# Attention and channel mix on one core: the scheduler books GpSimd with VectorE for some instructions, splits w_k out of PSUM and gets new prices

## The chip, the core and the metric

The kernel runs on one core of a Trainium2 chip. The metric is device time in microseconds (us) of the whole program, as the median of several runs. Engines are named as in the profile: PE is TensorE (PEld its weight load), DVE is VectorE, ACT is ScalarE, POOL is GpSimd, SP is SyncE, which only issues DMAs here. PSUM is the memory into which PE writes and which POOL's instructions in this kernel never touch; SBUF is the large one.

## What is computed

Causal attention with a forgetting bias, and behind it a channel mix with squared ReLU and a gate. Shapes: 8 batches, 8 heads, 576 positions, head width 64; model width 512, hidden width 1024.

```python
# attention, per batch and head
scores = scale * np.matmul(q, k.transpose(0, 1, 3, 2))
cum = np.cumsum(np.maximum(s, 0.0), axis=-1)
bias = -(cum[:, :, :, None] - cum[:, :, None, :])
scores = np.where(causal, -1e9, scores + np.minimum(bias, 0.0))
attn = np.exp(scores - max); attn = attn / (sum(attn) + 1e-09)
x = attn @ v                       # heads side by side: 512 wide
# channel mix on x
xk = mu_k * x + (1 - mu_k) * x_prev
xr = mu_r * x + (1 - mu_r) * x_prev
k = np.maximum(xk @ w_k, 0.0)
v = k * k @ w_v
out = v / (1 + np.exp(-(xr @ w_r)))
```

## The kernel before

**Precision.** Large products are made as sums of products of float16 parts: each operand is split into a high part and a low part (what the high part leaves), and three products (high by high, high by low, low by high) stand for one float32 product. The splits are the work of DVE, ACT and POOL around each product.

**Stages.** A visit is one batch and one pair of heads. The first eight visits treat batch 0 in two halves (four early visits A, then four Z); batch 1 follows in the same plain manner (`scores`, `turn_plain`, `sum_plain`), and from batch 2 on `split_scores`, `turn_by_dma` (weights are transposed by DMA) and `sum_values` are used. Between visits stand the 18 chunks of the channel mix (`channel_mix`, 256 tokens each): `hidden` (line 1954, products with w_k, then ReLU at 1968, and squares), `gate` (line 2031, products with w_r, tanh at 2045, scale at 2050) and `output` (line 2076, products with w_v, the last product with the gate at 2087).

**Squares.** In the first six chunks `hidden` makes kh = r*r (rounded) on ACT, squares r in place in float32 on ACT (line 1985) or on DVE (line 1990), and makes the low part kl on DVE from kh and r, both in SBUF (line 1996). In later chunks the exact square stays in PSUM (lines 2012 and 2018), so DVE's instruction for kl reads one operand from SBUF and one from PSUM.

**Weights.** The weights come as float64 words and are put together in `load_weight`: POOL extracts bits (lines 863, 871), ACT writes a first form to PSUM (878), DVE takes its maximum (883) and then writes the float32 weight to an SBUF tile `whole` (890; the tile's storage is named xrh or xrl). `split` makes the high part on ACT (901) or POOL (906) and the low part on DVE (914) or, in two instructions, on POOL (920 and 924); for w_v a third part, on ACT (933) or DVE (938). w_k has 8 such blocks, w_r 4, w_v 8.

**What sets the order.** Nothing is executed in the order of the source. Every instruction is added to a `Plan` with an engine, a price in ns, what it reads and writes, and a due time; `or_act`, `or_dve` and `or_pool` name a second engine for it. `forward` lays all instructions out on a clock of its own, engine by engine, taking for a free engine the ready instruction with the earliest due time; `backward` turns the result into new due times; this is repeated 60 times and the best layout is emitted. Each engine then executes its instructions strictly in that order, and real waits are made by semaphores. So a price never changes what an instruction costs on the chip; it changes where it stands and, with a second engine, on which it runs. For SP `forward` keeps a clock of the DMA rings (`moved`): FIRST and `land` are latencies, AHEAD says how far issue may run ahead of the transfers. While PE would have nothing to do early on, `one_idle` (line 464) puts dummy products in its queue.

## Time and profile before

| what | value |
|---|---|
| median of 3 runs | 773.28 us (772.52 to 773.45) |
| the profiled execution's own time | 774.11 us |
| its span, first to last instruction | 772.2 us |
| PE busy | 738.4 us, 96% |
| DVE, ACT, POOL busy | 607.2, 577.4, 504.1 us (79, 75, 65%) |
| matmuls | 5384 |
| instructions recorded | 16996 |

The profiled execution is one run; 1.9 us of its time lie outside the span. Busy time of PE is the union of its instructions with ends that are modelled, so that two matmuls that follow each other closely overlap; a PE that is shown busy can still be waiting for weights. The granted clock is a share of TensorE's full 2.4 GHz. In a view of waits, the engine and line named behind the arrow are what ended the idle time.

### The profile page before, as it was taken

The numbers are of one execution on the slowest core, as the hardware profiler recorded it, in microseconds if no ns is written. First come the engines' busy times: TensorE is split into PE (matmuls) and PEld (weight loads), VectorE is DVE, ScalarE is ACT, GpSimd is POOL, SyncE is SP. The second block draws the span as 40 slices with busy tenths as digits, with TensorE's granted clock in tenths as the row PEclk, the third lists the DMA queues.
The fourth block names the chain that finished last, engine by engine and source line by source line (L and its number), as shares of the span: only waits on it lengthen the run. The fifth ranks groups of instructions, "written<-read, shape, count | busy, mean of one in ns | idle before, by whom it ended". The sixth has DMA issues, their size and how long they took to land.

```text
span 772.2 us, 16996 instructions
## 1 busy us (share of the span) xinstructions
PE 738.4 (96%) x5384; PEld 492.7 (64%) x5384; DVE 607.2 (79%) x1820; ACT 577.4 (75%) x1751; POOL 504.1 (65%) x615
## 2 busy tenths in 40 slices
PE   8989998999899989999999999999999999999998
PEld 7867765765557555757575756575656666755665
DVE  8989978889878999888989898889998878413321
ACT  6989987878979897887888887988887777312311
POOL 6899999697365698777976887588758941100000
PEclk9999999999999999999999999999999999999999
DMA  8856672368258879788878788888787664200000
GB/s 269 259 180 185 198 216 95 99 158 179 71 104 185 176 170 159 158 174 168 174 175 167 177 174 166 163 173 177 173 144 163 105 115 65 67 28 14 14 28 27
DMA packets 207336, 109.91 MB, mean 142 GB/s; under 512 B 178000, under 2 KB 183888, under 8 KB 207248
## 3 DMA queue, kind: packets, MB, share of 16 engines
q1 hardware_dynamic: 207248, 108.85, 61.9%
q8 instruction: 42, 0.69, 0.4%
q14 instruction: 46, 0.38, 0.1%
HBM read 54.09 MB, written 12.24 MB: 86 GB/s over the span
## 4 chain that ended last, share of the span: by engine, by line
PE 37%; DVE 16%; ACT 15%; issue 6%; DMA 1%; POOL 1%; DVEq 0%; ACTq 0%; POOLq 0%
PE m L2076 10%; PE m L1954 7%; PE m L2031 5%; DVE W L1354 4%; ACT t L1323 3%; ACT W L1348 3%; PE pair L1482 3%; PE s L1296 2%; ACT s L1323 2%; DVE t L1308 2%; PE t L1296 2%; ACT wd L1527 2%; DVE s L1308 2%; PE s L1954 2%; PE t L1954 2%
## 5 line engine op out<-in xcount | busy, mean ns | idle before, releaser
L1954 PEld LDWEIGHTS <-w_k 128*128 128x128 f16 x1728 | 161.7, 98 | 37.7 <-issue 12.1
L1954 PE MATMUL m<-xkh,w_k 128*128 128x256 f16 x976 | 180.7, 275 | 2.5 <-DVE kl L2018 1.4
L2076 PE MATMUL m<-w_v,kh 128*128 128x512 f16 x528 | 167.9, 383 | 1.3 <-POOL w_v L924 0.7
L1954 PE MATMUL m<-xkl,w_k 128*128 128x256 f16 x488 | 134.3, 275 | 1.0 <-DVE xkl L1926 0.5
L2076 PE MATMUL m<-w_v,kl 128*128 128x512 f16 x264 | 100.2, 381 | 0.8 <-DVE kl L1996 0.7
L1143 POOL TENSOR_TENSOR KH<-raw,KH 64x576 fp32r<-64x576 f32 x64 | 93.5, 1461 | 4.7
L2076 PEld LDWEIGHTS <-kh 128*128 128x128 f16 x592 | 56.7, 98 | 57.7 <-issue 4.7
L2031 PE MATMUL m<-w_r,xrh 128*128 128x512 f16 x264 | 87.2, 386 | 2.6 <-ACT r L1968 1.3
L1167 POOL TENSOR_TENSOR QL<-raw,G 64x576 fp32r<-64x576 f32 (+1 forms) x64 | 86.2, 1347 | 3.3
L2050 POOL TENSOR_SCALAR g<-g,scale 128x512 f32<-128x512 f32 x26 | 20.8, 799 | 102.6 <-ACT g L2045 90.2
L1323 ACT ACTIVATE s<-s,nm 128x64 f32<-128x64 f32 (+2 forms) x144 | 61.5, 427 | 26.0 <-DVE nm L1308 20.7
L1296 PE MATMUL s<-KH,G 128*128 128x64 f32 (+3 forms) x192 | 68.8, 360 | 9.0 <-DVE W L1354 7.8
L1163 POOL CAST G<-raw 128x576 fp32r<-128x576 f32 x48 | 32.9, 686 | 65.1 <-issue 35.5
L1354 DVE SCALAR_TENSOR_TENSOR W<-s,rinv,W 128x64 f16<-128x64 f32 (+2 forms) x144 | 65.2, 456 | 11.4 <-ACT W L1348 10.0
L1348 ACT ACTIVATE W<-s,rinv 128x64 f16<-128x64 f32 (+2 forms) x144 | 65.0, 455 | 11.4 <-DVE rinv L1339 9.5
L1296 PE MATMUL s<-KL,QL 67*128 67x64 f32 (+3 forms) x192 | 66.5, 351 | 0.0
L1354 DVE SCALAR_TENSOR_TENSOR W<-t,rinv,W 128x320 f16<-128x320 f32 (+1 forms) x96 | 61.7, 646 | 5.6 <-ACT W L1348 4.9
L1323 ACT ACTIVATE t<-t,nm 128x320 f32<-128x320 f32 (+1 forms) x96 | 55.4, 577 | 7.2 <-DVE nm L1385 4.2
L1348 ACT ACTIVATE W<-t,rinv 128x320 f16<-128x320 f32 (+1 forms) x96 | 57.8, 608 | 2.2 <-DVE rinv L1339 2.1
L1308 DVE CUSTOM_DVE_ANT_0 t<-t,lower 128x320 f32<-128x320 f32 (+1 forms) x96 | 57.1, 599 | 1.9 <-PE t L1296 1.4
L1968 ACT ACTIVATE r<-m 128x512 f32<-128x512 f32 x57 | 34.1, 599 | 27.4 <-PE m L1954 21.8
L1482 PE MATMUL pair<-T,V 128*64 128x512 f16 (+6 forms) x768 | 54.4, 295 | 0.0
(260 smaller groups left out, 1968.5 us busy)
## 6 DMA issues: line engine op xcount, KB each, us to landing
raw<-in_q SPq DMA_DIRECT2D x112, 144.0 KB
raw<-in_k SPq DMA_DIRECT2D x32, 288.0 KB
vn<-in_v SPq DMA_DIRECT2D x24, 384.0 KB
out<-g SPq DMA_DIRECT2D x35, 256.0 KB
wd<-in_moe_w_v SPq DMA_DIRECT2D x8, 512.0 KB
T<-W SPq DMA_TRANSPOSE x192
V<-in_v SPq DMA_DIRECT2D x8, 320.0 KB
wd<-in_moe_w_k SPq DMA_DIRECT2D x4, 512.0 KB
```

Of the source, the lines that this page charges most:

```text
L1143: lambda own=own, other=other, K=K: nc.gpsimd.tensor_tensor(out=K.get()[other], in0=k.get()[own], in1=f32(K.get()[own]), op=ALU.subtract),
L1167: lambda x=x, QQ=QQ, QL=QL: nc.gpsimd.tensor_tensor(out=QL.get()[0:64, 0:nq], in0=x.get()[0:64], in1=f32(QQ.get()[0:64]), op=ALU.subtract,),
L1296: lambda x=x, G=G, K=K, r=r: nc.tensor.matmul(ps.get()[:m, :n], G.get()[:r, q : q + m], K.get()[:r, k0 : k0 + n], start=x == 0, stop=x == 1,),
L1308: lambda: nc.vector.tensor_tensor_reduce(out=ps.get()[:, :n], in0=ps.get()[:, :n], in1=mask(), scale=-SCALE, scalar=3.0e38, op0=ALU.add, o ...
L1323: lambda: nc.scalar.activation(ps.get()[:, :n], ps.get()[:, :n], AF.Exp, bias=nm.get()[:, i + o : i + o + 1], scale=-1.0, accum_out=sums.g ...
L1348: lambda: nc.scalar.activation(part(0), ps.get()[:, :n], AF.Copy, scale=rinv.get()[:, i : i + 1]),
L1354: lambda: nc.vector.scalar_tensor_tensor(out=part(1), in0=ps.get()[:, :n], scalar=rinv.get()[:, i : i + 1], in1=part(0), op0=ALU.mult, op1 ...
L1482: nc.tensor.matmul(ps.get()[64 * j : 64 * j + 64, a:e], V.get()[:, block[0], block[1], j], moving(j), start=first, stop=last, tile_positio ...
L1954: lambda u=u, f=f, c=c, n=n, w=w, x=x: nc.tensor.matmul(ps.get()[:, u * CT : (u + 1) * CT], weight["k", c, f // 4].get()[:, w, f % 4 * P : ...
L1968: lambda: nc.scalar.activation(r.get(), ps.get(), AF.Relu, scale=2.0**-26),
L2031: lambda c=c, n=n, x=x, w=w: nc.tensor.matmul(ps.get(), row(1, x, c, place + tt * P, place + tt * P + P), weight["r", c, 0].get()[:, w], s ...
L2076: lambda f=f, i=i, x=x, w=w, ps=ps, columns=columns: nc.tensor.matmul(ps.get()[:, 0:n], x.get()[:, f, ts], weight["v", f, 0].get()[:, w, c ...
```

## The change

The change leaves the arithmetic as it is, except in where w_k's float32 form is kept. It does five things.

1. `forward` gets a set `shared` of DVE instructions that read two operands from SBUF or run SBUF to SBUF in a fast mode. When one of them is next and POOL is booked (`free["POOL"] > s`), up to DEPTH ready DVE instructions are compared by due time plus the time that POOL is still booked, and the best goes first. A shared instruction then starts no earlier than POOL is free, and books POOL for its own length.
2. The members of that set lose the flat surcharge that stood for this before: line 1996 and 1990 had 400 ns, 914 had 450 ns.
3. For w_k the float32 form is written back to the PSUM bank (890), and both parts are split from there by ACT and DVE; POOL is no longer an alternative for w_k.
4. Prices of DMAs fall: plain transfers from 1.286 to 1.05 times the given ns, a transposing DMA from 195 to 155 ns a block, `land` from 1300 to 1150; ISSUE, FIRST and AHEAD are changed.
5. Prices of some DVE and ACT instructions are changed by tens of ns up to 130 ns.

```diff
-    ISSUE, FIRST, AHEAD = 500.0, 1000.0, 2500.0
+    ISSUE, FIRST, AHEAD = 520.0, 900.0, 3500.0
...
+        self.shared = set()
...
+            if e == "DVE" and i in self.shared and free["POOL"] > s:
+
+                some, aside = [(due[i], i)] if own == e else [], []
+                while some and ready[e] and len(some) < self.DEPTH:
+                    x = heapq.heappop(ready[e])
+                    if on[x[1]]:
+                        continue
+                    (some if self.tasks[x[1]][0] == e else aside).append(x)
+                    if len(aside) > 2:
+                        break
+                if some:
+                    best = min(
+                        some,
+                        key=lambda x: x[0]
+                        + (self.LOCK * (free["POOL"] - s) if x[1] in self.shared else 0.0),
+                    )
+                    for x in some + aside:
+                        if x is not best:
+                            heapq.heappush(ready[e], x)
+                    i = best[1]
...
+            if e == "DVE" and i in self.shared:
+                s = max(s, free["POOL"])
+                free["POOL"] = s + ns
...
+    LOCK = 1.0
...
-        return plan.add("SP", 1.286 * ns, emit, reads, writes, land=1300)
+        return plan.add("SP", 1.05 * ns, emit, reads, writes, land=1150)
...
-        whole = whole_in_ring(x) if name == "v" else wholes()
+        in_bank = name == "k"
+        whole = ps if in_bank else whole_in_ring(x) if name == "v" else wholes()
...
+            if in_bank:
+                act(
+                    lambda: nc.scalar.activation(
+                        block.get()[:, 0], ps.get(), AF.Copy, scale=unit_at
+                    ),
+                    [ps, key], [hi], 512, 94,
+                )
+                dve(
+                    lambda: nc.vector.scalar_tensor_tensor(
+                        out=block.get()[:, 1], in0=ps.get(), scalar=unit_at,
+                        in1=block.get()[:, 0], op0=ALU.mult, op1=ALU.subtract,
+                    ),
+                    [ps, key, hi], [lo], 512,
+                )
+                return
...
-            or_pool(dve(low, [whole, key, hi], [lo], 512, extra=450), low_in_two, 512, 1551)
+            or_pool(dve(low, [whole, key, hi], [lo], 512, extra=125, both=True), low_in_two, 512, 1551)
...
-        i = plan.add("SP", 195.0 * blocks, emit, reads, writes, land=1000)
+        i = plan.add("SP", 155.0 * blocks, emit, reads, writes, land=1000)
...
-                [lower, (corners_mask, 0), (corners_mask, 1)], [ps, (nm, i)], n, extra=78,
+                [lower, (corners_mask, 0), (corners_mask, 1)], [ps, (nm, i)], n, extra=137,
...
-                    2 * CT, 400,
+                    2 * CT, 75, both=True,
...
-                    [r, (kh, fp)], [(kl, fp)], 2 * CT, extra=400,
+                    [r, (kh, fp)], [(kl, fp)], 2 * CT, both=True,
...
-                lambda: scaled(nc.vector), DM,
+                lambda: scaled(nc.vector), DM, -75, both=True,
```

Because all due times follow from the layout, the order changes on every engine, from the first rows on. Work is the same apart from choices of engine: on DVE the in-place squares fall from 8 to 2 and the low parts of w_k go from 5 (914) to 8 (from PSUM); POOL loses the two-instruction low parts of w_k (3) and two of w_v, and gains 3 high parts of w_r; PE has the same products, with 93 dummy products for 84. Line numbers of the changed kernel are higher by up to 46: 838 is 868 there, 863 and 871 are 894 and 902, 1308 is 1354, 1354 is 1400, 1990 is 2036 and 1996 is 2042.

The first place is SP at the start of the program. in_s_t and in_s feed the bias, in_q and in_k the first scores, in_v the values, in_moe_w_k the weight w_k (512 KB a transfer). Before:

```order
L572 DMA vn_115<-in_s 64x576
L617 DMA g_121<-in_s_t 128x3x8
L838 DMA wd_127<-in_moe_w_k 128x1024
L2198 DMA xkh_129<-in_q 64x320
L2198 DMA xkl_144<-in_q 64x320
L1077 DMA KH_154<-in_k 128x320
L1019 DMA V_162<-in_v 128x384
L2198 DMA xkh_129<-in_q 64x320
L2198 DMA xkl_144<-in_q 64x320
```

And now:

```order
L868 DMA wd_115<-in_moe_w_k 128x1024
L868 DMA wd_121<-in_moe_w_k 128x1024
L647 DMA g_126<-in_s_t 128x3x8
L602 DMA vn_134<-in_s 64x576
L2244 DMA xkh_113<-in_q 64x320
L1123 DMA KH_156<-in_k 128x320
L2244 DMA xkl_154<-in_q 64x320
L868 DMA wd_167<-in_moe_w_k 128x1024
L868 DMA xrl_179<-in_moe_w_k 128x1024
```

Two transfers of w_k now stand ahead of everything, where one stood third; the first keys (in_k) stay sixth, with one more w_k transfer ahead of them.

The second place is POOL where the blocks of w_k are made (863 and 871 take the bits out of the words wd, xrl, xkh, xkl; 906 is a high part, 920 and 924 a low part). Before:

```order
L863 TENSOR_SCALAR w_k_00_340<-wd_237 128x512
L871 TENSOR_SCALAR w_k_00_340<-wd_237 128x512
L906 TENSOR_SCALAR w_k_00_377<-xrh_284,unit 128x512
L920 TENSOR_SCALAR xrh_284<-xrh_284,unit 128x512
L924 TENSOR_TENSOR w_k_00_377<-xrh_284,w_k_00_377 128x512
L863 TENSOR_SCALAR w_k_10_417<-xrl_303 128x512
L871 TENSOR_SCALAR w_k_10_417<-xrl_303 128x512
L863 TENSOR_SCALAR w_k_00_428<-xrl_303 128x512
L871 TENSOR_SCALAR w_k_00_428<-xrl_303 128x512
```

And now:

```order
L894 TENSOR_SCALAR w_k_10_390<-xkh_113 128x512
L902 TENSOR_SCALAR w_k_10_390<-xkh_113 128x512
L894 TENSOR_SCALAR w_k_00_422<-xkl_154 128x512
L902 TENSOR_SCALAR w_k_00_422<-xkl_154 128x512
L894 TENSOR_SCALAR w_k_10_466<-wd_115 128x512
L902 TENSOR_SCALAR w_k_10_466<-wd_115 128x512
L1205 CAST G_476<-raw_367 128x256
L1213 TENSOR_TENSOR QL_128<-raw_367,G_476 64x256
L2366 MEMSET xT_252 128x1
```

The three instructions of lines 906, 920 and 924 are gone from between the bit extractions, and preparation of queries (G and QL) stands earlier.

The third place is DVE in the fifth chunk's `hidden`, around the low part of its second pair of blocks (kl). 1308 is the masked minimum of a score tile, 1354 a low part of the attention weights, 1990 the in-place square. Before:

```order
L1354 SCALAR_TENSOR_TENSOR W_2247<-t_290,rinv_2360,W_2247 128x320
L1990 TENSOR_TENSOR r_110<-r_110 128x512
L1354 SCALAR_TENSOR_TENSOR W_2110<-s_174,rinv_2138,W_2110 128x448
L1996 SCALAR_TENSOR_TENSOR kl_1123<-kh_1036,r_110 128x512
L1308 ISA t_290,nm_249<-t_290,lower 128x320
L1308 ISA nm_249 128x1
L1400 TENSOR_REDUCE sums_187<-sums_187 64x2
```

And now:

```order
L810 RECIPROCAL scale_88<-scale_88 128x1
L1354 ISA t_313,nm_286<-t_313,lower 128x320
L1354 ISA nm_286 128x1
L1385 RECIPROCAL rinv_2217<-rinv_2217 128x1
L1354 ISA s_220,nm_248<-s_220,corners_mask 128x64
L1354 ISA nm_248 128x1
L2042 SCALAR_TENSOR_TENSOR kl_1104<-kh_1059,r_110 128x512
L1431 TENSOR_REDUCE nm_248<-nm_248 64x2
```

The square (1990, now 2036) no longer stands on DVE ahead of the low part; ACT makes it.

## Rows read from the trace of the kernel before

**Rows 1.** Page: the span; busy time by engine; the chain that ended last, by engine.

```profile
span 772.2 us, 16996 instructions
...
PE 738.4 (96%) x5384; PEld 492.7 (64%) x5384; DVE 607.2 (79%) x1820; ACT 577.4 (75%) x1751; POOL 504.1 (65%) x615
...
PE 37%; DVE 16%; ACT 15%; issue 6%; DMA 1%; POOL 1%; DVEq 0%; ACTq 0%; POOLq 0%
```

**Rows 2.** Windows of four stretches: us, busy time (x instructions) by engine, granted clock, DMA share, GB/s.

```profile
40.00:60.00 20.00, 16.54 (x122) 12.90 (x121) 17.39 (x62) 17.84 (x54) 19.18 (x24) 0.91 0.56 174
200.00:220.00 20.00, 16.79 (x83) 8.30 (x83) 17.95 (x54) 17.97 (x53) 10.88 (x12) 0.91 0.15 46
220.00:470.00 250.00, 240.59 (x1766) 154.15 (x1763) 220.48 (x663) 208.22 (x657) 190.61 (x213) 1.00 0.81 168
660.00:772.20 112.20, 109.09 (x741) 70.49 (x738) 30.66 (x45) 27.06 (x43) 8.09 (x10) 1.00 0.08 26
```

**Rows 3.** Chain that ended last, in order of time: start, us, engine, tile and line.

```profile
241.93 1.43 DVE kl L1996
...
255.41 1.27 DVE kl L1996
...
283.22 1.66 DVE kl L1996
...
288.75 1.23 DVE kl L1996
...
298.95 1.99 DVE kl L1996
...
456.30 1.52 DVE g L2050
```

**Rows 4.** Groups by form: line, engine, operation, out<-in, shapes, count | busy us, mean ns | idle before.

```profile
L1996 DVE SCALAR_TENSOR_TENSOR kl<-kh,r 128x512 f16<-128x512 f16 x24 | 26.6, 1106 | 0.5 <-ACT r L1985 0.4
...
L2018 DVE SCALAR_TENSOR_TENSOR kl<-kh,m 128x512 f16<-128x512 f16 x37 | 25.2, 680 | 0.8
...
L1990 DVE TENSOR_TENSOR r<-r 128x512 f32<-128x512 f32 x8 | 10.3, 1289 | 1.2 <-ACT kh L1981 1.2
...
L1985 ACT ACTIVATE r<-r 128x512 f32<-128x512 f32 x16 | 10.2, 638 | 0.1
...
L914 DVE SCALAR_TENSOR_TENSOR w_k<-xrh,unit,w_k 128x512 f16<-128x512 f32 x5 | 5.6, 1110 | 0.0
```

**Rows 5.** Line 2050: count, duration ns min/median/max, first and last start us.

```profile
L2050 DVE TENSOR_SCALAR g<-g,scale x6: 531/887/1667, 175.8 to 537.1; 128x512 f32<-128x512 f32 x6
```

**Rows 6.** Line 924, same columns.

```profile
L924 POOL TENSOR_TENSOR w_k<-xrh,w_k x3: 1157/1159/1595, 18.5 to 39.9; 128x512 f16<-128x512 f32 x3
```

**Rows 7.** VectorE in order of time, 294 to 302 us: start, us, line, operation, out<-in.

```profile
294.70 0.68 DVE L1996 SCALAR_TENSOR_TENSOR kl<-kh,r 128x512 f16<-128x512 f16 x1
...
298.87 2.07 DVE L1996 SCALAR_TENSOR_TENSOR kl<-kh,r 128x512 f16<-128x512 f16 x1
```

**Rows 8.** GpSimd in the same stretch.

```profile
293.32 1.28 POOL L1572 TENSOR_TENSOR xkl<-wd,xkh 128x576 f16<-128x576 f32 x1
295.44 0.76 POOL L2050 TENSOR_SCALAR g<-g,scale 128x512 f32<-128x512 f32 x1 [0.84 <-ACT g L2045]
...
298.75 1.63 POOL L1069 TENSOR_TENSOR V<-vn,V 128x768 f16<-128x768 f32 x1
300.46 1.74 POOL L1143 TENSOR_TENSOR KH<-raw,KH 64x576 fp32r<-64x576 f32 x1
```

**Rows 9.** Windows of the first 20 us, columns as in group 2.

```profile
0.00:10.00 10.00, 8.09 (x66) 7.65 (x67) 8.01 (x17) 4.83 (x10) 8.14 (x37) 1.00 0.70 194
10.00:20.00 10.00, 9.38 (x80) 8.26 (x81) 8.60 (x34) 7.80 (x31) 6.05 (x8) 1.00 1.03 352
```

**Rows 10.** TensorE: the first score product against loaded keys.

```profile
8.35 0.78 PE L1212 MATMUL s<-KH,xkh 128*128 128x192 f32 x4
```

**Rows 11.** Waits from 40 to 58 us: us in total, times, longest us.

```profile
PEld s L1223 <- POOL KH L1143: 1.3, 2, 1.1
```

More of the change, by code (lines that the diff above doesn't have):

```diff
@@ L405, in act, with dve @@
         )
-    def dve(emit, reads, writes, n, rate=0.96, extra=70, quarters=(0, 0)):
-        return at_quarters(plan.add("DVE", n / rate + extra, emit, reads, writes), quarters)
+    def dve(emit, reads, writes, n, rate=0.96, extra=70, quarters=(0, 0), both=False):
+        i = plan.add("DVE", n / rate + extra, emit, reads, writes)
+        if both:
+            plan.shared.add(i)
+        return at_quarters(i, quarters)
     def pool(emit, reads, writes, n, extra, rate=0.8333, quarters=(0, 0)):
@@ L414, in or_act, with or_dve @@
         plan.or_on(i, "ACT", n * 0.8333 + extra, emit)
-    def or_dve(i, emit, n, extra=70):
-        plan.or_on(i, "DVE", n / 0.96 + extra, emit)
+    def or_dve(i, emit, n, extra=70, both=False, rate=0.96):
+        plan.or_on(i, "DVE", n / rate + extra, emit)
+        if both:
+            plan.shared.add(i)
     def or_pool(i, emit, n, extra=150):
@@ L886, in load_weight @@
             ),
-            [], [ps, (top, at)], 512, extra=210,
+            [], [ps, (top, at)], 512, extra=135,
         )
@@ L893, in load_weight @@
             ),
-            [(last3, 0), (last3, 1), ps], [whole], 512,
+            [(last3, 0), (last3, 1)] + ([] if in_bank else [ps]), [whole], 512,
         )
@@ L941, in split @@
                     ),
-                    512,
+                    512, 155, both=True, rate=3.84,
                 )
@@ L1035, in greatest @@
             ),
-            [vn], [(am, hp)], P * nk, extra=120,
+            [vn], [(am, hp)], P * nk, extra=60,
         )
@@ L1583, in mix_pair @@
                         pool(lambda f=low: f(nc.gpsimd), [src] + his, los, n, 210, 2.0),
-                        lambda f=low: f(nc.vector), n, 180,
+                        lambda f=low: f(nc.vector), n, both=True,
                     )
@@ L1884, in mixed @@
                     ),
-                    parts(*z[:2]) + [share_key(z)], [(xm, ("a", *z))], z[2], 290,
+                    parts(*z[:2]) + [share_key(z)], [(xm, ("a", *z))], z[2], 160,
                 )
@@ L1906, in mixed @@
                     parts(*z[:2]) + [share_key(z)] + [(xm, ("a", *u)) for u in todo],
-                    [(xm, ("d", *z))], z[2], extra=250 if z is not todo[-1] else 130,
+                    [(xm, ("d", *z))], z[2], extra=135,
                 )
```

## Prediction

> **What bounds the kernel now.** I read the page's first and fourth parts, then the windows, then the chain. PE is busy 738.4 of 772.2 us [rows 1], so at most some 34 us of visible idle time are to be had, and only where PE lacks work. The windows say where that is. From 660 us on attention is over, DVE and ACT are busy 31 and 27 of 112 us, and PE works without a gap for all but the last drain [rows 2]: this end is a fixed 109 us, and no order shortens it. From 220 to 470 us PE is busy 240.6 of 250, DVE 220.5, ACT 208.2, at full clock [rows 2]: three engines are nearly full, and the chain of the whole run lies 37% on PE, 16% on DVE and 15% on ACT [rows 1]. There a late DVE result can cost PE time. The two bad stretches are 40 to 60 us and 200 to 220 us: PE is busy 16.5 and 16.8 of 20 us and is granted 0.91 of full speed [rows 2]. In both, DVE and ACT are busy about 17 to 18 of 20. So the total is PE's work, plus what PE loses while other engines prepare its operands, plus a fixed end; the change can move only the middle part.
>
> **Part 1, booking GpSimd with VectorE.** The kl instruction of line 1996 takes 1106 ns on average in 24 instances, against 680 for line 2018, which does the same on as many elements but has one operand in PSUM [rows 4]. The instances say why. At 294.70 us one took 0.68 us [rows 7]: POOL had ended an instruction at 294.60 and began the next at 295.44 [rows 8]. At 298.87 us one took 2.07 us [rows 7], with a POOL instruction running from 298.75 to 300.38 [rows 8]; 300.94 less 300.38 is 0.56 us, so DVE did its work only after POOL had ended. POOL's next one, begun at 300.46 inside DVE's share, took 1.74 us [rows 8]. Both engines lose, and which loses more depends on who begins first.
>
> The rule behind it is in the Trainium skill, "SBUF — State Buffer", section "Who interferes with whom": a VectorE instruction with two SBUF inputs and a GpSimd instruction that reads SBUF exclude each other for the whole instruction, and the order of issue decides who blocks. The trace agrees, with 0.68 against 2.07 us [rows 7]. The same rule speaks against this change: a layout made beforehand helps only as far as engines meet on the chip in the booked order.
>
> What it costs now: 24 x (1106 - 680) = 10.2 us at line 1996 and 8 x (1289 - 680) = 4.9 us at line 1990 [rows 4]. Most of that lies beside other work. What lies on the path is in the chain: five pieces of line 1996 of 1.43, 1.27, 1.66, 1.23 and 1.99 us, less 0.68 each, are 4.2 us, and the gate's scale on DVE stood there with 1.52 us [rows 3] where its fastest instance took 0.53 [rows 5], 1.0 us more. Together 5.2 us. The ends are 0 (the order is booked, but engines meet otherwise) and -5.2. Six of the eight in-place squares go to ACT, 6 x 0.64 = 3.8 us [rows 4] on an engine with 42 us to spare from 220 to 470 us [rows 2]; I cost that at nothing, covered by that idle time, and at up to 3.8 us where ACT leads. I take -4.0 us: six of the instructions leave DVE whatever the timing, and the rest can be placed beside them.
>
> **Part 2, w_k from PSUM.** DVE makes 8 low parts at 0.68 (the PSUM form, line 2018) in place of 5 at 1.11 [rows 4]: 5.4 for 5.6 us, nothing. POOL loses three instructions of 1.16 us [rows 6] with their first halves and two high parts. What waited for POOL around there: weight loads of scores waited 1.3 us for a key preparation between 40 and 58 us [rows 11]. So the ends are 0 and -1.3; I take -0.5. A bank is held longer, from the bit form to the end of the split, but chunk 0 needs the banks only after w_k is done.
>
> **Part 3, the order of the first loads.** Two w_k transfers go first, where one stood third, so the first keys have 512 KB more ahead of them. At 194 GB/s, the rate of the first 10 us, that is 2.7 us; at 352 GB/s, the rate of the second 10 us, 1.5 us [rows 9]. The first product with keys ran at 8.35 us [rows 10]; dummy products fill PE until then. In exchange bit extraction and maxima of w_k come when DVE and ACT are busy only 8.0 and 4.8 of 10 us [rows 9]. Ends: 0 and +2.7; I take +0.5, nearer to 0, since what DVE and ACT do earlier for w_k is off their backs when the scores come.
>
> **Part 4, the new prices.** They change no duration, only the order everywhere. How far a new order alone can move the time I read from the worst stretch: 200 to 220 us lost 3.2 us of PE and 0.09 x 20 = 1.8 us of clock [rows 2], 5.0 us in all. One such hole may close or open: ends -5.0 and +5.0, and I take 0.
>
> **Sum.** -4.0 - 0.5 + 0.5 + 0 = -4.0 us. The profiled execution took 774.1 us (772.2 of span and 1.9 around it), which would become 770.1. It lies 0.8 us above the median of 773.28, so the forecast is 769.3.
>
> **Rivals.**
> - *A hole closes too.* With DVE freed and chunk 0's products with w_k standing earlier on PE, the stretch of 200 to 220 us fills: 5.0 us more, 764.3. For it: POOL is busy only 10.9 of 20 us there [rows 2], so what starves PE is order, not volume. Against it: DVE and ACT are at 18 of 20 in it.
> - *The booking doesn't meet the chip.* Real waits shift DVE against POOL by more than the 0.68 us that such an instruction takes, so line 1996 stays near 1.1 us; parts 2 and 3 cancel. Time 773.3. By the skill's rule on issue order ("SBUF — State Buffer", as above) this is what a misplaced order gives.
> - *Transfers are booked too short.* A transposing DMA is priced at 155 ns a block for 195, other loads at 1.05 for 1.286, about a fifth less, while DMAs already take 0.81 of their engines from 220 to 470 us [rows 2]. If turned weights land later than booked, the value products (line 1482) stand at the head of PE's queue and everything behind them waits, since PE executes in order. Its price is a hole as above, 5.0 us, with the first loads' full 2.7 us and half of part 1 lost to it: 773.3 + 5.0 + 2.7 - 2.0 = 779.0. It decides once turned weights land after PE has used up the channel-mix products that stand ahead of the value products. Against it: PE was busy 240.6 of 250 us there, and more issue ahead gives transfers more time.
>
> **How the numbers follow.** Forecast 769.3 with chance 0.42, hole closing 764.3 with 0.16, no effect 773.3 with 0.17, transfers too short 779.0 with 0.25. About 0.2%, 1.5 us, is what a measurement of this kernel can tell from no change. So faster 0.58, same 0.17, slower 0.25. For the range, all lower ends give 774.1 - 5.2 - 1.3 - 5.0 = 762.6, or 761.8 against the median, and the upper side reaches to the slow rival, 779.0; a little outside on the low side as DVE's stalls beside the chain may count too: 761 to 779.
>
> **What would show it.** Line 1996 (2042 there) should fall from 1106 to under 900 ns, and line 1990's count to 2; both would show part 1 at work. Pieces of kl over 1.2 us should be gone from the chain. PE's busy time in windows from 220 to 470 us should grow from 0.96. The first product with keys should come at about 10 us, two later. Waits of PE for turned weights, or a POOL queue that stands behind a gate for many us, would show the slow rival. The forecast is wrong if PE loses more in 40 to 60 or 200 to 220 us than before, or if kl is as long as it was.

## The result: slower by 0.66%, with more than that lost behind one instruction

| kernel | median, us | ratio to the kernel before |
|---|---|---|
| before, timed beside it | 773.45 | 1 |
| after | 778.29 | 1.0066 (1.0048 to 1.0083) |

The forecast was 769.3 and faster. The time lies inside its range (761 to 779), its sign was wrong. The first part of the page after, and its groups for the lines of [rows 4, 5]; the columns of a group are count, then shortest, middle and longest duration in ns:

```profile
span 776.3 us, 17034 instructions
PE 735.7 (95%) x5393; PEld 493.4 (64%) x5393; DVE 611.7 (79%) x1823; ACT 577.5 (74%) x1753; POOL 493.6 (64%) x605
```
```profile
L2042 DVE SCALAR_TENSOR_TENSOR kl<-kh,r x24: 679/894/1745, 66.1 to 332.3; 128x512 f16<-128x512 f16 x24
L2036 DVE TENSOR_TENSOR r<-r x2: 939/975/1011, 141.3 to 146.5; 128x512 f32<-128x512 f32 x2
L2096 DVE TENSOR_SCALAR g<-g,scale x8: 578/1526/1779, 242.7 to 656.1; 128x512 f32<-128x512 f32 x8
L2096 DVE TENSOR_SCALAR g<-g,scale_t x2: 545/1892/3240, 377.9 to 577.1; 128x512 f32<-128x512 f32 x2
L1618 DVE TENSOR_TENSOR xkl<-wd,xkh x5: 741/897/7354, 269.9 to 604.2; 128x576 f16<-128x576 f32 x2, 128x128 f16<-128x128 f32 x1, 128x320 f16<-128x320 f32 x1, 128x384 f16<-128x384 f32 x1
```

PE's work is the same; its idle time grew. The kl instruction has a mean of 1006 ns over its 24 instances, where it was 1106 [rows 4]. The line that stands out is the last: one low part of the channel mix, line 1618, took 7354 ns. The windows after, as [rows 2] (columns: span, busy time and count of PE, PEld, DVE, ACT and POOL, granted clock, DMA share, GB/s):

```profile
40.00:60.00 20.00, 18.12 (x147) 13.62 (x147) 18.55 (x84) 17.96 (x61) 17.86 (x28) 1.00 0.76 248
180.00:200.00 20.00, 17.74 (x123) 12.75 (x122) 17.00 (x54) 17.63 (x57) 12.72 (x20) 0.91 0.74 156
200.00:220.00 20.00, 19.10 (x104) 10.06 (x101) 18.78 (x57) 18.19 (x58) 11.03 (x12) 1.00 0.30 85
260.00:280.00 20.00, 14.66 (x120) 10.55 (x119) 17.60 (x58) 16.22 (x54) 12.39 (x16) 1.00 0.78 171
440.00:460.00 20.00, 12.72 (x88) 8.06 (x89) 17.51 (x30) 8.82 (x29) 12.19 (x13) 0.83 0.55 127
444.00:445.00 1.00, 0.00 (x0) 0.00 (x0) 1.00 (x1) 0.00 (x0) 1.00 (x2) 0.50 0.00 0
```

Both bad stretches of before are better: PE gains 1.6 us in 40 to 60 us and 2.3 us in 200 to 220 us against [rows 2]. But the second has a like 20 us earlier: from 180 to 200 us PE is now busy 17.74 of 20 us at a clock of 0.91, where it was busy 19.66 us at full clock. Two new ones stand at 260 and 440 us. In the last DVE is busy 17.5 of 20 us with 30 instructions, and PE, idle since 439.5 us, is at the lower clock level (0.50) by 444.

To see what each stretch costs, I gave every product its columns times a fixed price (half for the products with 64 columns of weights, which run in pairs), added these up in order, and asked when the two traces reach the same sum. Products stand in another order in the two traces, so one such figure alone is good to about 1 us. By this the kernel after is ahead by 4.6 us at 160, 4.1 at 180, 6.0 at 260, 1.8 at 280, 5.0 at 340 and 2.5 at 440 us. At 460 us it is 6.3 us behind, and it ends 3.7 behind. So one event costs 8.8 us. Here it is, DVE first (start, duration, engine, line, operation), then POOL, then who waited from 438 to 449 us (total, times, longest):

```profile
439.27 0.16 DVE L1385 RECIPROCAL rinv<-rinv 128x1 f32<-128x1 f32 x1
439.34 7.35 DVE L1618 TENSOR_TENSOR xkl<-wd,xkh 128x320 f16<-128x320 f32 x1
446.62 0.22 DVE L1354 CUSTOM_DVE_ANT_0 s<-s,corners_mask 128x64 f32<-128x64 f32 x1
```
```profile
439.16 0.67 POOL L1618 TENSOR_TENSOR xkl<-wd,xkh 128x256 f16<-128x256 f32 x1
439.78 0.82 POOL L1113 CAST V<-vn 128x768 f16<-128x768 f32 x1
440.59 0.90 POOL L1107 TENSOR_SCALAR vn<-vn,scale 128x768 f32<-128x768 f32 x1
441.45 1.63 POOL L1115 TENSOR_TENSOR V<-vn,V 128x768 f16<-128x768 f32 x1
443.03 0.82 POOL L1113 CAST V<-vn 128x768 f16<-128x768 f32 x1
443.84 0.90 POOL L1107 TENSOR_SCALAR vn<-vn,scale 128x768 f32<-128x768 f32 x1
444.71 1.64 POOL L1115 TENSOR_TENSOR V<-vn,V 128x768 f16<-128x768 f32 x1
```
```profile
PE s L1342 <- DVE W L1400: 7.7, 1, 7.7
ACT nm L1439 <- DVE nm L1354: 6.3, 1, 6.3
```

DVE began while POOL's subtraction ran, and was still not done when six more POOL instructions (the splits of the values of two heads) had followed it without a gap, none of them stretched. It ended 0.35 us after the last. I call such an instruction **caught**. Behind it in DVE's queue stood the maxima and weights that ACT and then PE needed.

### The profile page after: what moved, and what is told of

It is laid out like the page before. It is cut to its first block, busy times and chain, and to the rows that moved or that the text cites. A ratio compares the mean times of both kernels' runs of the same rounds, so it can differ in the third digit from the quotient of the medians.

```text
span 776.3 us, 17034 instructions
## 1 busy us (share of the span) xinstructions
PE 735.7 (95%) x5393; PEld 493.4 (64%) x5393; DVE 611.7 (79%) x1823; ACT 577.5 (74%) x1753; POOL 493.6 (64%) x605
## 5 line engine op out<-in xcount | busy, mean ns | idle before, releaser
L1342 PE MATMUL s<-KH,G 128*128 128x64 f32 (+2 forms) x192 | 69.3, 363 | 14.0 <-DVE W L1400 13.0
L1394 ACT ACTIVATE W<-s,rinv 128x64 f16<-128x64 f32 (+1 forms) x144 | 64.9, 456 | 11.7 <-DVE rinv L1385 9.3
L1400 DVE SCALAR_TENSOR_TENSOR W<-s,rinv,W 128x64 f16<-128x64 f32 (+1 forms) x144 | 65.2, 457 | 9.6 <-ACT W L1394 8.8
L1342 PE MATMUL s<-KL,QL 67*128 67x64 f32 (+2 forms) x192 | 65.2, 345 | 0.0
L1342 PEld LDWEIGHTS s<-KH,G 128*128 128x128 f32 (+1 forms) x192 | 34.5, 180 | 33.4 <-DVE W L1400 25.4
```

Source lines behind the costliest of these rows:

```text
L1342: lambda x=x, G=G, K=K, r=r: nc.tensor.matmul(ps.get()[:m, :n], G.get()[:r, q : q + m], K.get()[:r, k0 : k0 + n], start=x == 0, stop=x == 1,),
L1394: lambda: nc.scalar.activation(part(0), ps.get()[:, :n], AF.Copy, scale=rinv.get()[:, i : i + 1]),
L1400: lambda: nc.vector.scalar_tensor_tensor(out=part(1), in0=ps.get()[:, :n], scalar=rinv.get()[:, i : i + 1], in1=part(0), op0=ALU.mult, op1 ...
```

## Experiments: the caught instruction

**The same order, that one instruction on POOL** (its second engine in the plan):

```diff
+            if name in self.FLIP:        # {("low", 4, 3, 256)}: batch 4, piece from 256
+                on[i] = self.tasks[i][0]
```

> The changed kernel in its own order, instruction for instruction, but the one subtraction of line 1618 that ran on DVE for 7.35 us from 439.34 us (low part of the channel mix, batch 4, piece from 256, 320 columns) is emitted on POOL, at the same place of the order. Theory A (that one instruction stood behind seven of POOL's and PE lost its lead of 2.5 us there and 6 us more): the time comes back by 7 to 10 us, to 768 to 771 us, under the kernel before (773.4). PE's idle time of 7.70 us at 447 us is gone, and nothing of DVE lasts over 3.3 us. Rival B (the new order or the shorter booked transfers cost it, and the hole would open at another place): 776 to 779 us. Rival C (the instruction was late for another reason than POOL, such as its operands): it takes as long on POOL, the wait of 7 us stays and the time stays at 778.

Measured: 769.53 us, ratio 0.9954 (0.9942 to 0.9965). Theory A. By the sums of products it runs beside the kernel after to 440 us (3.0 ahead of before), is 2.5 ahead at 460 and 5.2 at the end. C falls too: on POOL the instruction ran without a wait, so its operands were there.

**The instruction stays on DVE, and POOL waits for it.**

```diff
+                        f(nc.vector)
+                        if (b, c, o) == (4, 3, 256):
+                            nc.gpsimd.tensor_copy(mark[:, 0:1], own(1)[:, 0:1])
```

> The changed kernel in its own order with one instruction more: right behind the caught subtraction (line 1618, batch 4, piece from 256, still on DVE) POOL copies one column of its result, so POOL's run of the values' splits begins only when DVE is done. Theory A (DVE was caught because POOL's run never let go of the port): the subtraction takes 0.4 to 1.2 us, PE's idle time of 7.7 us is gone and the time is 768 to 771 us, as where it ran on POOL. Rival B (DVE was held by something else, and POOL only ran beside it): it still takes some 7 us, POOL's copy waits as long, and the time is 778 us or more. Rival C (the time of the run where it stood on POOL came from DVE having less to do): 0.4 to 1.2 us for the subtraction, but the time stays over 774.

Measured: 768.67 us, 0.9924 (0.9901 to 0.9946). DVE's instruction, POOL around it, and the window:

```profile
436.89 0.83 DVE L1620 TENSOR_TENSOR xkl<-wd,xkh 128x320 f16<-128x320 f32 x1
```
```profile
436.71 0.66 POOL L1620 TENSOR_TENSOR xkl<-wd,xkh 128x256 f16<-128x256 f32 x1
437.79 0.19 POOL L1633 COPY mark<-xkl 128x1 f16<-128x1 f16 x1 [0.41 <-DVE xkl L1620]
437.91 0.83 POOL L1115 CAST V<-vn 128x768 f16<-128x768 f32 x1
```
```profile
440.00:460.00 20.00, 19.96 (x128) 11.07 (x127) 17.10 (x53) 15.36 (x50) 19.34 (x22) 1.00 0.88 166
```

0.83 us for 7.35, though DVE began 0.18 us into POOL's subtraction in both kernels: DVE waits for that to end at 437.37 and is done. PE is busy 19.96 of 20 us where it was 12.72. Nothing was taken away; POOL has one instruction of 0.19 us more. That the run of POOL's was the cause is shown.

**The gate's scales on POOL as well.**

```diff
+FLIP = {("low", 4, 3, 256)} | {("gate", c, t) for c in range(2, 14) for t in range(2)}
```

> As the first run (the caught subtraction on POOL), and the gate's scales of chunks 2 to 13 that stood on DVE are emitted on POOL as well, at the same places; one of them had been caught for 2.9 to 3.2 us at 378 us, the others took 1.4 us each on average against 0.53 alone. Theory A (each caught or stretched scale costs the chain something): under the first run's 769.5 by 1 to 4 us, 766 to 769. Rival B (off the path, or POOL's later gates keep the outputs waiting): 769 to 773, no gain.

Measured: 769.12 us, 0.9923 (0.9901 to 0.9944). Its base is the first run, 0.9954 (0.9942 to 0.9965): the intervals just meet, so the times alone show no gain. The two traces do, at the place. In the first run a scale is caught for 2.89 us at 377.86 us, and PE stands still for want of weights behind it:

```profile
382.25 0.35 PE L1347 MATMUL s<-KH,G 128*128 128x192 f32 x1 [1.93 <-DVE W L1405]
```

With the scale on POOL that gap is gone. PE is busy 10.00 us from 380 to 390 us, for 8.07, and by the sums of products the run goes from 1.0 us behind the first at 380 us to 1.1 ahead at 385. So this catch cost about 2 us. The profiled execution had lost 3.6 us to the first run by 40 us, long before the first moved scale, and this hides most of it in its total. A scale of 4.75 us in a kernel below cost next to nothing. A catch costs only what is queued behind it.

## Experiments: the parts alone, and orders without any part

**A small shift of the planner**, `GAP = 170.0` to `180.0`, in both kernels.

> The changed kernel with one number of the planner moved that nothing in the hardware depends on (the gap that makes it put in dummy products, 170 to 180 ns), so that the whole order is drawn anew under the same rules. It has the three parts of the change, but instructions meet elsewhere. Theory A (a chance meeting of one DVE instruction with a run of POOL's costs 9 us, the rest of the change gains): 768 to 773 us where no such meeting falls on the chain, 777 to 780 where one does, and the trace shows which. Rival B (the change as such costs 5 us): 776 to 780 us whatever the meetings.

Measured: 779.6 us, 1.0078 (1.0052 to 1.0105). The orders of DVE, ACT and POOL are those of after, row by row, and line 1618 is caught again, at 439.63 for 7.35 us. So the event belongs to the order and not to one execution.

> The kernel before with the same one number moved (170 to 180 ns), so the order is drawn anew by the old rules. It prices how far a new order alone moves the time. Theory A: some 2 to 6 us to either side of 773.4 (768 to 779), with longest DVE instructions under 2.2 us as in the kernel before. Rival B (orders are worth less than 1.5 us): 772 to 775.

Measured: 773.29 us, 1.0005 (0.9993 to 1.0018). DVE's order was the same row by row, so this says little of new orders.

**One part alone, on the kernel before**: the booking (with its prices and marks), the prices of transfers, and w_k from PSUM. The fifth item of the change, prices of single DVE and ACT instructions, was not run alone.

```diff
+            if e == "DVE" and i in self.shared:          # booking
+                s = max(s, free["POOL"])
+                free["POOL"] = s + ns
-    ISSUE, FIRST, AHEAD = 500.0, 1000.0, 2500.0          # transfers
+    ISSUE, FIRST, AHEAD = 520.0, 900.0, 3500.0
+        in_bank = name == "k"                            # w_k
+        whole = ps if in_bank else whole_in_ring(x) if name == "v" else wholes()
```

> The kernel before with the booking alone: the marks of instructions that take the port, GpSimd's time moved behind them, their shorter prices. w_k as before, the planner's prices of transfers as before. The forecast's part 1 says -4.0 us (0 to -5.2), so 769.7 against 773.7, with the new order's own 5.0 to either side. Theory A (booking gains what was forecast, where no DVE instruction is caught behind a run of POOL's): 768 to 772 and no DVE instruction over 2.2 us; 5 to 9 us more where one is caught, and the trace shows it. Rival B (booking gains nothing on the chip): 773 to 775 without any such instruction.

Measured: 773.84 us, 1.0003 (0.9986 to 1.002). Neither theory fits well. It has a catch (a gate's scale, 4.75 us at 443), but its lead hardly fell there (5.1 us at 440, 4.8 at 460). It lost it from 500 to 560 us (5.4 to 2.9) and from 640 to 680 (3.8 to 1.3). I did not follow these up.

> The kernel before with the planner's new prices of transfers alone (issue 520 for 500, first 900 for 1000, ahead 3500 for 2500, loads at 1.05 for 1.286 of their base, landing 1150 for 1300, turned weights 155 for 195 a block). The forecast's parts 3 and 4 say +0.5 (0 to +2.7) and 0 (5 to either side), so 774 against 773.7. Theory A (the prices cost little, the one caught instruction was the loss): 772 to 776. Rival B (turned weights and key rows come too late by the short prices): 777 to 782, with PE's waits for value products and for DMA in its longest idle times.

Measured: 772.8 us, 0.9978 (0.9963 to 0.9992). Theory A.

> The kernel before with the first change of w_k alone: its high and low parts are made from the PSUM bank without the copy to SBUF. The forecast's part 2 says -0.5 (0 to -1.3), so 773.2 against 773.7 (772.4 to 773.7), with what the new order adds to either side. Theory A: within 1.5 us of the kernel before. Rival B (the bank held longer keeps chunk 0 or the scores waiting): 775 to 778, with PE idle more than before in the first 60 us.

Measured: 769.35 us, 0.9933 (0.9913 to 0.9952): some nine times what was expected, and below what either theory said. It is 3.9 us ahead at 120 us and 9.2 at 220.

**New orders of the kernel before without any part.** One planner number each, which prices no instruction: a weight load that PE would wait for counts 140 for 150; an instruction is offered to its second engine 330 for 300 ns later.

> The kernel before with one number of the planner moved that prices no instruction (a weight load that PE would wait for counts 140 for 150), which draws the whole order anew by the old rules: DVE's order agrees with that of before to 0.30, as little as with the single parts of the change (0.20 to 0.31). It prices a new order by itself, where a first try had left the order as it was. Theory A (most of what the single parts gained is the hole of 200 to 220 us, which nearly any new order closes): 768 to 773, with PE busy over 18 of 20 us there. Rival B (the parts gained by what they do): 773 to 777 and the hole stays, 16.5 to 17.5 of 20.

Measured: 780.22 us, 1.0065 (1.0046 to 1.0083).

> As the run before, with another number (how much later an instruction may be offered to its second engine, 330 for 300 ns): DVE's order agrees with that of before to 0.27. Theory A: 768 to 773, the hole of 200 to 220 us closed. Rival B: 773 to 777 and the hole stays. The distance of the two orders from each other and from the kernel before is what an order by itself is worth here.

Measured: 777.31 us, 1.0034 (1.002 to 1.0049).

Both came out outside what either theory said. From 200 to 220 us PE is busy 18.99 and 18.85 of 20 us in them, and 18.54 to 19.45 in the three parts alone, all at full clock, for 16.79 at 0.91 [rows 2]. But a hole can also stand next to its old place. These are the windows of 180 to 220 us, in the order before, after, booking, transfers, w_k, first drawn-anew order, second:

```profile
180.00:220.00 40.00, 36.45 (x219) 21.69 (x218) 35.69 (x111) 35.90 (x111) 19.59 (x28) 0.96 0.41 98
180.00:220.00 40.00, 36.83 (x224) 22.81 (x222) 35.77 (x110) 35.82 (x113) 23.76 (x32) 0.96 0.52 120
180.00:220.00 40.00, 37.82 (x229) 22.74 (x228) 35.89 (x112) 34.57 (x115) 17.06 (x19) 1.00 0.50 104
180.00:220.00 40.00, 35.26 (x220) 21.20 (x219) 36.48 (x116) 35.22 (x111) 16.30 (x18) 1.00 0.41 103
180.00:220.00 40.00, 39.43 (x263) 25.03 (x262) 35.76 (x110) 33.73 (x102) 25.50 (x32) 1.00 0.51 112
180.00:220.00 40.00, 38.41 (x241) 23.58 (x241) 34.82 (x107) 34.82 (x109) 18.57 (x29) 1.00 0.45 99
180.00:220.00 40.00, 38.16 (x233) 22.80 (x231) 35.89 (x108) 34.62 (x109) 18.59 (x25) 1.00 0.42 102
```

The booking, w_k and both drawn-anew orders close the hole: PE has 1.4 to 3.0 us more than before, at full clock. With the prices of transfers alone, as in the kernel after, another stands 20 us earlier (PE is busy 15.81 of 20 us from 180 to 200 us). All five are ahead of the kernel before, by 1.7 to 5.8 us at 180 us and by 4.5 to 9.2 us at 220 us. What the two drawn-anew orders lost, they lost later. The first, DVE and POOL:

```profile
276.05 8.37 DVE L1996 SCALAR_TENSOR_TENSOR kl<-kh,r 128x512 f16<-128x512 f16 x1
284.35 0.67 DVE L1354 SCALAR_TENSOR_TENSOR W<-s,rinv,W 128x448 f16<-128x448 f32 x1
```
```profile
275.84 0.66 POOL L1149 CAST KL<-raw 64x576 fp32r<-64x576 f32 x1
276.48 1.78 POOL L1061 TENSOR_SCALAR vn<-vn,scale 128x768 f32<-128x768 f32 x2
278.22 1.59 POOL L1067 CAST V<-vn 128x768 f16<-128x768 f32 x2
279.78 3.22 POOL L1069 TENSOR_TENSOR V<-vn,V 128x768 f16<-128x768 f32 x2
282.98 0.90 POOL L1061 TENSOR_SCALAR vn<-vn,scale 128x768 f32<-128x768 f32 x1
```
```profile
PE s L1296 <- DVE W L1354: 7.8, 1, 7.8
ACT r L1968 <- DVE kl L1996: 7.1, 1, 7.1
```

A kl caught through eight instructions, and PE idle 7.8 us. The order goes from 4.4 us ahead at 280 to 3.0 behind at 300. The second has a kl of 5.11 us at 282.79.

**Is the catch what they lost?** The remedy of above in these orders, behind the caught kl:

```diff
+                    low_kls.append(0)
+                    if len(low_kls) == 17:        # then: in (17, 18); in the second order: == 18
+                        nc.gpsimd.tensor_copy(mark[:, 0:1], kl.get()[:, 2 * fp, 0:1])
```

> The kernel before in the order of the first drawn-anew run (780.2 against 774.3), with one instruction more: behind its caught kl instruction (line 1996, 8.37 us from 276.05) POOL copies one column of the result and so waits for it. In POOL's queue the copy stands ahead of the key cast that DVE met there. Theory A (the catch is what that order lost: it was 4.4 us ahead of the kernel before at 280 us and 3.0 behind at 300): the time falls by 5 to 8 us, to 772 to 775, and the instruction takes 0.7 to 1.3 us. Rival B (that order is slow for other reasons, the catch is covered): 778 to 780 although the instruction is short.

Measured: 781.43 us, 1.0118 (1.0095 to 1.0142), no gain. The instruction took 1.21 us, but the next kl, begun at 279.79, was caught for 6.10 us by the same run of POOL's. That told the theories not apart, so:

> The first drawn-anew order of the kernel before (780.2 against 774.3), with POOL's copy, and so its wait, behind both kl instructions that the same run of POOL's can catch (8.37 us in that order, and 6.10 us of the next one when only the first had a wait). Theory A (the catch is what that order lost): both take 0.7 to 2.1 us and the time falls by 4 to 8 us, to 772 to 776. Rival B (the order is slow for other reasons): 778 to 781 although both are short.

Measured: 773.48 us, 0.9985 (0.9972 to 0.9998), from 1.0065. The kl instructions and the window of 280 to 300 us, without the waits and with both:

```profile
277.50 0.85 DVE L1998 SCALAR_TENSOR_TENSOR kl<-kh,r 128x512 f16<-128x512 f16 x1
281.31 1.05 DVE L1998 SCALAR_TENSOR_TENSOR kl<-kh,r 128x512 f16<-128x512 f16 x1
```
```profile
280.00:300.00 20.00, 14.93 (x112) 10.07 (x113) 15.88 (x37) 12.60 (x40) 10.28 (x10) 0.83 0.42 100
```
```profile
280.00:300.00 20.00, 19.60 (x137) 11.62 (x136) 17.16 (x47) 16.68 (x50) 19.03 (x21) 1.00 0.64 153
```

> The second drawn-anew order of the kernel before (777.3 against 774.3), with POOL's copy behind its one caught kl instruction (5.11 us from 282.79); in POOL's queue it stands one instruction of the run later, so DVE still waits for that one. Theory A: the instruction takes 1.5 to 2.5 us and the time falls by 2.5 to 5 us, to 772 to 775 (that order was 4.3 us ahead of the kernel before at 280 us and 1.6 behind at 300). Rival B: 776 to 778.

Measured: 774.9 us, 0.9999 (0.9986 to 1.0012), from 1.0034; the kl took 1.85 us. Theory A in both, in full in the first order. The second still falls back by 2.8 us from 280 to 300 us. DVE's next low part meets POOL's subtraction of 1.63 us there, and PE stands still for 2.9 us, until the weights that DVE makes behind it:

```profile
298.14 2.18 DVE L1574 TENSOR_TENSOR xkl<-wd,xkh 128x576 f16<-128x576 f32 x1 [0.48 <-POOL xkh L1571]
```

**The fastest order with the remedy**, w_k alone, behind its low part of 3.24 us at 621 us:

> The kernel before with the change of w_k alone (769.35 against 774.1), with the same remedy behind its caught subtraction (128x576, 3.24 us from 620.98). That order's lead over the kernel before fell from 8.1 to 5.8 us there. Theory A: 1.5 to 2.5 us less, 767 to 768. Rival B (the catch stood beside other work, or the copy costs POOL as much): 769 to 770.

Measured: 767.13 us, 0.9925 (0.9909 to 0.9941). The instruction took 1.64 us. The median is 2.2 us lower, but the intervals of 0.9933 and 0.9925 overlap, so the times show no gain. In the traces, by the sums of products, the run with the wait gains 1.6 us on the other from 620 to 628 us. This and the changed kernel with one wait (0.9924) or with its scales on POOL (0.9923) are the fastest seen.

## Experiments: what decides a catch

Three sets of small trials let DVE meet POOL's instructions in the kernel's forms, with the start of DVE's shifted.

> No part of the kernel: only small trials, and zeros are written as output. In each trial DVE starts one instruction with two SBUF operands (the subtraction of 320 columns of line 1618, the kl form of 512, the gate's scale of 512, the kl form with one operand in PSUM) after a delay of 0 to 0.5 us, while POOL works through a run of up to seven of the kernel's instructions that wait for nothing, or through one kind of them alone, or through a run in which each has a wait that was met long before. Theory A (DVE can stand behind a whole run of POOL's): in some trials DVE's subtraction takes 3 to 8 us where it takes 0.35 alone; the trials tell which forms and which start decide. Theory B (as in the forecast: DVE gets in when POOL's current instruction ends, whatever follows): never over 2.1 us, and POOL's next instruction is stretched. Theory C (only with waits between POOL's instructions does DVE get in): the run whose instructions each have a wait shows under 2.1 us and the run without waits 5 to 8 us. The kl form with an operand in PSUM should take 0.68 us throughout by all three.

> No part of the kernel: small trials, and zeros are written as output. As the first trials, but POOL's run is the one of 437 to 446 us of the changed kernel, in its order (values of two heads in turn, so that none of its instructions waits for the one before it), or the one of 377 us (key casts, then low parts), and DVE's instruction comes right behind a reciprocal of one column, as in both places, or behind a copy of one column from PSUM. DVE's start is shifted in steps of 0.1 us over the first two instructions of the run. Theory A (what decides is that POOL's instructions follow each other without a gap, so that it never gives the port away): the subtraction of 320 columns takes 2 to 8 us in a good part of the trials, behind the reciprocal and behind the copy. Theory B (the reciprocal ahead of it decides): 2 to 8 us behind the reciprocal alone, under 2.1 us behind the copy. Theory C (neither; something else of the kernel at that moment decides): under 2.1 us throughout, and POOL's next instruction is stretched by what DVE takes.

> No part of the kernel: small trials, and zeros are written as output. 35 trials of seven meetings each: POOL works through 14 instructions that wait for nothing (subtractions, scalings, casts of two heads in turn), DVE beside it through copies in PSUM of varying length, each time followed by one instruction with two SBUF operands or the gate's scale. Seven trials with nothing beside, seven with ACT copying in SBUF, seven with PE multiplying, seven with both, seven with both and four stores to DRAM. Theory A (work of other engines makes POOL keep the port): catches of 2 us and more in the groups with that work and none in the first. Rival B (chance, at any phase, once in some dozens of meetings): a few catches in all groups. Rival C (neither): none over 2.2 us in 245 meetings, and what decides stays open.

The subtraction in the second set, then DVE's three forms in the third:

```profile
L69 DVE TENSOR_TENSOR xkl<-wd,xkh x50: 471/736/1478, 9.9 to 629.9; 128x320 f16<-128x320 f32 x50
```
```profile
L69 DVE TENSOR_TENSOR xkl<-wd,xkh x88: 466/782/1973, 11.8 to 602.6; 128x320 f16<-128x320 f32 x88
L74 DVE TENSOR_SCALAR g<-g,sc x77: 523/803/2009, 20.5 to 595.1; 128x512 f32<-128x512 f32 x77
L88 DVE SCALAR_TENSOR_TENSOR xkl<-xkh,wd x80: 673/1051/2033, 10.0 to 600.8; 128x512 f16<-128x512 f16 x80
```

In the first set the subtraction took at most 1.12 us. No trial has a catch: not with POOL's run in the order of 439 us, not behind the reciprocal that stood ahead of DVE's instruction there, not with work on ACT, PE and DMA beside. In the 16 traces of the kernel in its variants, 545 such DVE instructions on SBUF alone (kl, in-place square, gate's scale, low part from SBUF) began while a POOL instruction had 0.1 us or more to go, and 17 of these took over 2.2 us. A POOL run without a gap is not enough. In the second drawn-anew order a kl begun at 277.79 took 0.87 us: it got in when POOL's current instruction ended, and POOL's next one was stretched from 0.66 to 1.11 us. The next kl, at 282.79, met the same unbroken run and stood behind five instructions for 5.11 us. Nor does a catch always last to the end of the run: the scale of 3.24 us at 377.92 in the kernel after got in with POOL's run still going on. What decides is **not settled**.

## Why the prediction was wrong

- **The step that failed is part 1's price of a meeting.** From [rows 7, 8] it took that DVE waits until POOL's current instruction has ended, and so gave the ends 0 and -5.2, with no loss. The runs show 7.35 us behind seven instructions, 8.8 us of lead lost, and all of it back with one wait. None of the 17 long ones lasted longer than POOL's run without a gap and DVE's own work, so that run is the upper end that these traces show. The step did say that engines may meet otherwise than booked, but its price for that was no gain, not a loss. The plan has POOL's run behind DVE's instruction; no semaphore tells POOL so.
- **Part 1's gain is not shown.** Kl fell from 1106 to 1006 ns, not under 900. In the kernel before 39 of 50 such instructions began while POOL was at work, after the change 32 of 41, the same share. Booking alone gave 1.0003. Kl in the chain, the second sign, can't be read: the chain after goes back only to 606 us. PE's busy share from 220 to 470 us, the third, fell from 0.96 to 0.92, and is 0.95 with the one wait. The rival "the booking doesn't meet the chip" described the mechanism best, though not the time.
- **Without the one event the time is 768.7 to 769.5, where the forecast was, but for another reason. That is luck.** The rival "a hole closes too" did not come true in this kernel either: from 180 to 220 us one hole takes the place of another, and 4.1 us of the lead were there at 180 us. Most of it is made from 100 to 140 us (0.5 to 5.0 us), where the forecast named no gain. The windows before and after:

```profile
110.00:130.00 20.00, 17.89 (x124) 12.37 (x123) 15.85 (x51) 16.30 (x46) 19.00 (x23) 0.91 0.29 93
110.00:130.00 20.00, 19.80 (x157) 14.50 (x157) 18.77 (x68) 19.69 (x66) 15.35 (x25) 1.00 0.59 181
```

  Which part does that is not shown. The parts alone and the drawn-anew orders all gain there too, 0.9 to 4.6 us from 100 to 140 us.
- **Part 2** was mis-sized if taken alone: -0.5 forecast, about -5 measured (0.9933). How much of that is w_k and how much the new order is open; its 9.2 us at 220 are 2 to 3 more than the two drawn-anew orders have there (7.2 and 6.3).
- **Part 3** held at its end, not on the way. The first product with keys came at 9.67 us for 8.35 [rows 10], as forecast about 10. The lag was 4.7 us at 40 us, more than the end of 2.7, and gone at 60. The prices of transfers alone show the same (3.9 and 0.1), so it is theirs. (Two executions in the one order of the changed kernel, the first run and the one with the scales on POOL, lag by 3.6 and 7.2 us at 40 us.)
- **Part 4** had the right size for the wrong place. An order drawn anew, without any part, was worth +0.65% and +0.34%, about +5.0 and +2.6 us. Each is a hole closed early and a catch later.
- **The slow rival**, transfers booked too short, is there in small. In the kernel before PE never stood still for over 0.1 us ahead of a value product. In the kernel after it did for 2.2 us in all, most of it here, until a turn issued at 260.12 us had landed at 263.23:

```profile
263.32 1.00 PE L1528 MATMUL pair<-T,V 128*64 128x512 f16 x8 [1.84 <-issue]
```

  The view names no releaser; the semaphore on which TensorE's weight loads waited there is that turn's. With the prices of transfers alone such gaps add up to 0.3 us. So that is about 2 us of the 5.0 priced, and not shown to come from the prices. The lead that falls by 4.2 us from 260 to 280 us is 5.1 us again at 320. The rival's time, 779.0, was near the result by another mechanism.

## What to carry to other kernels

Where two engines share a port, bound a wait by the longest run without a pause that the other engine can have, and look what stands in the queue behind the waiting instruction. A planner that books a shared resource has to make the order real where a run follows: here one copied column, 0.19 us, was worth 8 to 9 us. A hole that is gone from its window may stand in the next one, so compare a wider stretch before calling it closed. And when a change redraws a whole order, time two orders redrawn for no reason beside it, since these alone moved the time by 3 and 5 us.

## What the runs showed of the hardware

A DVE instruction with two SBUF operands can stand behind up to eight POOL instructions (8.37 us), and so can the gate's scale, which reads one tensor (4.75 us behind five). The Trainium skill ("SBUF — State Buffer", section "Who interferes with whom") has the engine that issues first hold the shared ports for its whole instruction while the other blocks. One meeting agrees with that (0.83 us above); in the catches DVE stayed out through two to eight POOL instructions in a row, and there the measurement decides. A wait of POOL's that depends on DVE's result ended it each time, and once the next DVE instruction was caught by the same run.
